# One exponential of 128x512 in place of four of 128x128, with the maxima subtracted on VectorE, in the first batch of an attention and expert-layer kernel

## Chip, core and metric

The kernel runs on one core of a Trainium2 chip. The metric is the device time of one execution in microseconds. TensorE (PE), VectorE (DVE), ScalarE (ACT), GpSimd (POOL) and SyncE (SP) run their own instruction queues in order and wait for one another by semaphores. Tiles lie in SBUF, results of TensorE in PSUM, in eight banks of 128 x 512 floats.

## The reference

```
x       = q, k times 64 ** -0.25                    # (4 batches, 8 heads, 576 rows, 64)
phi(x)  = exp(h - max(h)),  h = x @ omega.T - |x|^2/2    # 128 features, max over the features
kv, z   = sum over rows of phi(k) * v,  of phi(k)
attn    = phi(q) @ kv / (phi(q) @ z + 1e-6)
x       = attn as 2304 x 512
h = x @ w_in;  x = (h * clip(h + 3, 0, 6) / 6) @ w_out       # 512 -> 2048 -> 512
h = x @ w2_in; y = (h * sigmoid(1.702 h)) @ w2_out
```

The term |x|^2/2 is the same for all features of a row, so it falls out of h - max(h). The kernel therefore takes only the projection, its maximum over 128 features, and the exponential of the difference.

## The kernel before

The attention of one batch is a list of steps (`att_steps`, from L450). For each of eight heads: PJ (L330) projects 512 rows of k and q onto the features, PL (L313) does the same once per batch for the 64 leftover rows of all heads, QT (L366) transposes the query features on TensorE and copies them out (in batch 0 on VectorE, L372; later on ScalarE), KV (L341) sums phi(k) v into a bank that ScalarE copies to the tile `kv` (L363), NU (L377) multiplies the query features with kv (L386, L395) and normalizes on VectorE (`den`, `rden`, `xt`, L413 to L421), and XT (L429) transposes the result (L433) and splits it into a rounded high part on ScalarE (L279) and the rest on VectorE (L280).

A projection writes two banks, one for each half, each of 128 rows x 4 groups x 128 features (`project`, L282). `features` (L293) then takes the maximum over the features of each group, negated, on VectorE (L295), and makes four exponentials on ScalarE, one per group with its maximum as the bias (L297), from PSUM into the SBUF tile `e` (or `el` for the leftover rows). Both PJ and PL call it once per half. It gives back the last exponential and the reduction; the first weight conversion of the run is issued behind those of heads 4 and 5 (`att.feat`, L745), later ones behind `gate` or behind those of head 7.

Batch 0 runs alone at the start (L742). Its last twelve steps share the time with the first weight conversions: `convert_1` (L200) unpacks 64-bit weights by two ScalarE activations (L213, L215), three VectorE operations (`wmag`, `wtop`, `wpow`, L217 to L225) and one GpSimd product (L228); `convert_2` (L231) adds the parts on VectorE (L236) and splits them (L239, L240). Then the loop over chunks of the first expert layer begins (L807): `emit_h` (L513) and `emit_o` (L555) are TensorE's main work, the steps of batches 1 to 3 are put between them by `side`, and the second layer follows (`h_pair`, L856; `o_pair`, L1008).

The instructions of each engine are ordered by a planner that lists them by a timeline of its own costs, in order of emission where several are ready; only `behind` fixes an order by hand. An instruction at the head of an engine's queue that waits holds up all behind it.

Of the kernel before, what the change touches and what calls it, by code (L numbers as in the profile page):

```python
# [14 lines left out]
AF = mybir.ActivationFunctionType  # L15
ALU = mybir.AluOpType
AX = mybir.AxisListType
# [5 lines left out]
def performer_moe_kernel(  # L23
# [13 lines left out]
    nc = tc.nc  # L37
# [4 lines left out]
    B, NPAIR, P = qk.shape[:3]  # L42
# [3 lines left out]
    M = omega.shape[1]  # L46
# [62 lines left out]
    def bank(shape, name):  # L109
        n_ps[0] += 1  # L110
        if banks[0] == "acc" or banks[0] == "both" and n_ps[0] % 2:
            return acc.tile(shape, F32, tag="acc", name="acc")
        return psp.tile(shape, F32, tag="ps", name="ps")
# [84 lines left out]
    half = {}  # L198
# [47 lines left out]
    whole = {}  # L246
# [35 lines left out]
    def project(a, ps):  # L282

        last = None
        for n in range(4):
            for half in (1, 0):
                rows = HALVES[half]
                with behind(last):
                    last = nc.tensor.matmul(  # L289
                        out=ps[half][:, n, :], lhsT=a(rows, n), rhs=omt[rows, :], start=True, stop=True  # L290
                    )

    def features(ps, e):  # L293
        mx = at.tile([P, 4], F32, tag="mx", bufs=4, name="mx")
        dve = nc.vector.reduce_max(mx, ps, axis=AX.X, negate=True)  # L295
        for r in range(4):
            act = nc.scalar.activation(  # L297
                out=e[:, r, :], in_=ps[:, r, :], func=AF.Exp, bias=mx[:, r:r + 1]
            )
        return act, dve  # L300

    class Att:
# [10 lines left out]
        def PL(self):  # L313
            a, self.vl = lqkv.pop(self.b)
            self.el = at.tile([P, 2 * NPAIR, M], F32, tag="el", name="el")
            ps = [bank([P, NPAIR, M], "ps") for _ in HALVES]
            project(lambda rows, i: a[rows, i, :], ps)
            for j, p in enumerate(ps):
                features(p, self.el[:, j * NPAIR:(j + 1) * NPAIR])

        def QTL(self):
            ps = bank([P, NPAIR, P], "ps")
# [7 lines left out]
        def PJ(self, h):  # L330
            a = qkv[self.b, h // 2][0][:, h % 2]
            ps = [bank([P, R, M], "ps") for _ in HALVES]
            project(lambda rows, n: a[rows, n // 2, n % 2, :], ps)
            self.e[h] = at.tile([P, 2, R, M], F32, tag="e", bufs=2, name="e")
            for half, p in enumerate(ps):
                self.feat[h] = features(p, self.e[h][:, half])

        def feature(self, h, j, r):
            return self.e[h][:, r % 2, 2 * j + r // 2]
# [344 lines left out]
    ps = bank([P, 4, P], "ps")  # L684
    for n in range(WARM):
        nc.tensor.matmul(
            out=ps.rearrange("p a m -> p (a m)"),
# [557 lines left out]
```

## Time and profile before

| what | us |
|---|---|
| median of 3 runs (lowest, highest) | 902.18 (901.68, 904.79) |
| profiled execution | 906.58 |
| its span, first to last instruction | 904.8 |
| PE, DVE, ACT, POOL busy in the span | 886.0, 554.3, 478.0, 322.6 |

Times in views count from the span's first instruction. In a timeline a row gives start, duration, engine, line, operation, tiles, shape and count; in brackets stands how long the engine had been idle and what released it. A duration runs to the last write, and the next instruction of an engine can start a little before it ends, so the difference of two starts is what an instruction takes of its queue. Rows with a count are several merged. The busy time of PE is modelled. The granted clock of TensorE was 0.998 over the span.

### The profile page before, as it was taken

Reading aid. Unit: us, or ns where it says so; the run is one execution under the profiler, and the core shown is the slowest. Engines: PE = TensorE matmul, PEld = TensorE weight load, DVE = VectorE, ACT = ScalarE, POOL = GpSimd, SP = SyncE. Lnnn points to the kernel's source line nnn. Section 1 sums busy time; section 2 is a strip of 40 time slices with the busy share of each in tenths; the row PEclk is TensorE's granted clock in tenths of the full one; section 3 lists DMA queues with packets and bytes.
Section 4 is the critical chain, followed back from the end, with each engine's and each line's share of the span. In section 5 each row is a group of like instructions: output and inputs, shape, how many; then the busy total and the mean of one; then the engine's idle time right before and its main releaser. Section 6 shows DMA issues by size and latency. Waiting matters only on the chain.

```text
span 904.8 us, 16525 instructions
## 1 busy us (share of the span) xinstructions
PE 886.0 (98%) x6344; PEld 757.1 (84%) x6344; DVE 554.3 (61%) x952; ACT 478.0 (53%) x973; POOL 322.6 (36%) x257
## 2 busy tenths in 40 slices
PE   8899999999999999999999999999999999999998
PEld 6667777788788778878888888878999888899998
DVE  5887688473754736475573343666887343368785
ACT  5887677376664666656553343444545232245452
POOL 0122222044636565475673121877000243440000
PEclk9999999999999999999999999999999999999999
DMA  6677669698888987778857325999889644565562
GB/s 209 226 248 270 234 239 316 245 329 282 286 275 288 342 304 290 233 276 288 314 204 256 128 98 206 349 400 356 277 288 354 233 170 162 180 174 153 158 204 82
DMA packets 74416, 224.57 MB, mean 248 GB/s; under 512 B 7521, under 2 KB 13793, under 8 KB 74337
## 3 DMA queue, kind: packets, MB, share of 16 engines
q1 hardware_dynamic: 73872, 223.12, 71.1%
q8 instruction: 50, 0.82, 0.4%
q10 hardware_dynamic: 464, 0.39, 0.2%
q14 instruction: 30, 0.24, 0.1%
HBM read 160.57 MB, written 62.91 MB: 247 GB/s over the span
## 4 chain that ended last, share of the span: by engine, by line
PE 82%; DVE 8%; ACT 6%; issue 1%; POOL 1%; DMA 1%; DVEq 0%; SPq 0%; ACTq 0%; POOLq 0%
PE o L1008 19%; PE o L555 18%; PE ps L513 18%; PE h L856 16%; PE hl L873 3%; PE ps L289 2%; ACT e L297 2%; DVE w L236 2%; PE ps L386 1%; PE ps L347 1%; ACT wtop L213 1%; DVE mx L295 1%; DVE wtop L221 1%; PE ps L369 1%; DVE gs L530 1%
## 5 line engine op out<-in xcount | busy, mean ns | idle before, releaser
L513 PE MATMUL ps<-x,wss 128*128 128x512 f32 x768 | 195.5, 399 | 2.5 <-ACT el L297 1.1
L1008 PE MATMUL o<-wss,gs 128*128 128x256 f32 x1512 | 173.9, 277 | 0.2 <-DVE gs L977 0.2
L1008 PEld LDWEIGHTS o<-wss,gs 128*128 128x128 f32 x1512 | 173.4, 188 | 0.9 <-DVE gs L977 0.6
L513 PEld LDWEIGHTS ps<-x,wss 128*128 128x128 f32 x768 | 140.9, 189 | 35.0 <-ACT wss L239 3.1
L856 PE MATMUL h<-xo,wss 128*128 128x512 f32 x672 | 158.5, 391 | 0.9 <-DVE t L889 0.9
L856 PEld LDWEIGHTS h<-xo,wss 128*128 128x128 f32 x672 | 123.9, 188 | 27.5 <-DVE t L889 1.8
L228 POOL TENSOR_TENSOR w<-w,wpow 128x1024 f32<-128x1024 f32 x32 | 69.2, 2162 | 204.6 <-DVE wpow L225 166.7
L525 DVE SCALAR_TENSOR_TENSOR ga<-ga,ps 128x512 f32<-128x512 f32 x80 | 50.1, 632 | 121.1 <-ACT ga L524 121.1
L899 POOL TENSOR_TENSOR g<-g,c 128x512 f32<-128x512 f32 x48 | 64.7, 1349 | 164.0 <-ACT g L898 163.8
L976 ACT CAST gs<-g 128x512 fp32r<-128x512 f32 x112 | 69.6, 622 | 80.3 <-PE o L1008 49.3
L555 PE MATMUL o<-gs,wsh 128*128 128x512 f32 (+1 forms) x480 | 110.4, 374 | 1.2 <-ACT gs L529 1.0
L555 PE MATMUL o<-gs,wss 128*128 128x512 f32 (+1 forms) x480 | 109.5, 374 | 0.2 <-ACT gs L529 0.2
L253 POOL TENSOR_TENSOR wsn<-w,wsn 128x512 fp32r<-128x512 f32 x64 | 86.6, 1367 | 63.5 <-ACT wsn L252 63.5
L977 DVE TENSOR_TENSOR gs<-g,gs 128x512 fp32r<-128x512 f32 x112 | 79.9, 716 | 33.6 <-ACT gs L976 32.3
L524 ACT ACTIVATE ga<-ps,three 128x512 f32<-128x512 f32 x80 | 51.4, 650 | 86.5 <-PE ps L513 86.0
L555 PEld LDWEIGHTS o<-gs,wsh 128*128 128x128 f32 x480 | 82.2, 188 | 17.6 <-ACT gs L529 1.4
L555 PEld LDWEIGHTS o<-gs,wss 128*128 128x128 f32 x480 | 82.4, 188 | 15.8 <-ACT gs L529 0.4
L297 ACT ACTIVATE e<-ps,mx 128x128 f32<-128x128 f32 x220 | 61.1, 396 | 23.5 <-DVE mx L295 23.3
L530 DVE TENSOR_TENSOR gs<-ga,gs 128x512 fp32r<-128x512 f32 x80 | 62.5, 791 | 16.5 <-ACT gs L529 14.7
L898 ACT ACTIVATE g<-c 128x512 f32<-128x512 f32 x48 | 30.3, 632 | 60.2 <-DVE c L889 60.2
L529 ACT CAST gs<-ga 128x512 fp32r<-128x512 f32 x80 | 46.0, 580 | 27.8 <-DVE ga L525 27.4
L252 ACT CAST wsn<-w 128x512 fp32r<-128x512 f32 x64 | 38.3, 620 | 39.5 <-DVE w L236 13.2
(132 smaller groups left out, 1102.7 us busy)
## 6 DMA issues: line engine op xcount, KB each, us to landing
wss<-left SPq DMA_DIRECT2D x56, 512.0 KB, 3.9
wss<-ws0i SPq DMA_DIRECT2D x48, 512.0 KB, 4.9
wraw<-in_w_in_dram SPq DMA_DIRECT2D x32, 512.0 KB, 5.4
wraw<-in_w_out_dram SPq DMA_DIRECT2D x32, 512.0 KB, 6.3
left<-wsn SPq DMA_DIRECT2D x32, 512.0 KB, 3.7
wss<-ws0o SPq DMA_DIRECT2D x24, 512.0 KB, 4.6
ws0i<-wss SPq DMA_DIRECT2D x16, 512.0 KB, 3.3
wss<-sumsa SPq DMA_DIRECT2D x16, 512.0 KB, 3.5
```

The costliest lines, as they stand in the source:

```text
L228: nc.gpsimd.tensor_tensor(out=w, in0=w, in1=q, op=ALU.mult)
L253: nc.gpsimd.tensor_tensor(out=s[:, :, 1], in0=t, in1=s[:, :, 0].bitcast(F32), op=ALU.subtract)
L297: act = nc.scalar.activation(out=e[:, r, :], in_=ps[:, r, :], func=AF.Exp, bias=mx[:, r:r + 1])
L513: nc.tensor.matmul(out=ps, lhsT=w[:, wi, kk, :], rhs=x[:, xi, kk, :], start=(m == 0), stop=(m == 3 * NK - 1),)
L524: nc.scalar.activation(out=g, in_=ps, func=AF.Relu, bias=three)
L530: gate[1] = nc.vector.tensor_tensor(out=s[:, 1, :], in0=g, in1=s[:, 0, :].bitcast(F32), op=ALU.subtract)
L555: nc.tensor.matmul(out=ps[:, e, :], lhsT=w[:, wi, cols], rhs=s[:, gi, :], start=(c == 0 and m == 0 and e == 0), stop=(c == NC - 1 and m == ...
L856: nc.tensor.matmul(out=ps, lhsT=s[:, wi, q, :], rhs=xop[q, op][:, xi], start=(first and m == 0), stop=(m == 5), skip_group_check=not first,)
L899: mul = eng.tensor_tensor(out=g, in0=g, in1=src, op=ALU.mult)
L976: split_ins[0] = nc.scalar.copy(hi, g)
L977: split_ins[1] = nc.vector.tensor_tensor(out=lo, in0=g, in1=hi.bitcast(F32), op=ALU.subtract)
L1008: last_row[0] = nc.tensor.matmul(out=out, lhsT=s[:, gi, d * P:(d + 1) * P], rhs=w[:, wi, :], start=(start and m == 0), stop=(stop and m == 2),
```

## The change

In batch 0, for the second half of every projection (eight heads and the leftover rows), the reduction no longer negates, VectorE subtracts the broadcast maxima from the whole bank into the SBUF tile, and ScalarE makes one exponential of 128x512 there, in place. The first halves, and all of batches 1 to 3, stay as they are. What `features` gives back is then that exponential and the subtraction.

```diff
-    def features(ps, e):
+    def features(ps, e, whole=False):
         mx = at.tile([P, 4], F32, tag="mx", bufs=4, name="mx")
+        if whole:
+            nc.vector.reduce_max(mx, ps, axis=AX.X)
+            dve = nc.vector.tensor_tensor(
+                out=e, in0=ps, in1=mx.unsqueeze(2).to_broadcast([P, 4, M]), op=ALU.subtract
+            )
+            return nc.scalar.activation(out=e, in_=e, func=AF.Exp), dve
         dve = nc.vector.reduce_max(mx, ps, axis=AX.X, negate=True)
         for r in range(4):
...
             for j, p in enumerate(ps):
-                features(p, self.el[:, j * NPAIR:(j + 1) * NPAIR])
+                features(p, self.el[:, j * NPAIR:(j + 1) * NPAIR], self.b == 0 and j == 1)
...
             for half, p in enumerate(ps):
-                self.feat[h] = features(p, self.e[h][:, half])
+                self.feat[h] = features(p, self.e[h][:, half], self.b == 0 and half == 1)
```

## Rows read from the trace of the kernel before

**Rows 1.** Page, part 1: engine, busy us, share of the span, instructions.
```profile
PE 886.0 (98%) x6344; PEld 757.1 (84%) x6344; DVE 554.3 (61%) x952; ACT 478.0 (53%) x973; POOL 322.6 (36%) x257
```

**Rows 2.** Busy time by stretch: stretch, its length, busy us of each engine, clock, DMA.
```profile
5.28:42.00 36.72, 30.84 (x459) 25.39 (x458) 27.06 (x64) 27.21 (x88) 2.14 (x1) 1.00 0.67 226
42.00:60.00 18.00, 15.95 (x125) 11.21 (x126) 16.29 (x36) 14.24 (x30) 5.43 (x3) 1.00 0.83 279
60.00:80.00 20.00, 20.00 (x144) 16.18 (x143) 14.93 (x27) 17.31 (x40) 5.27 (x3) 1.00 0.66 229
```

**Rows 3.** The chain of waits in order of time: start us, us, what.
```profile
29.55 2.15 POOL w L228
...
53.28 0.73 PE ps L513 x2
```

**Rows 4.** Waits of PE from 0 to 60 us: us in total, times, longest.
```profile
PE acc L386 <- ACT kv L363: 3.0, 3, 1.5
...
PE acc L433 <- DVE den L413: 1.5, 2, 0.8
...
PE acc L289 <- ACT e L297: 0.6, 1, 0.6
```

**Rows 5.** Timeline of ScalarE, 0 to 60 us.
```profile
8.14 1.14 ACT L297 ACTIVATE e<-ps,mx 128x128 f32<-128x128 f32 x4 [6.13 <-DVE mx L295]
9.15 1.16 ACT L297 ACTIVATE e<-acc,mx 128x128 f32<-128x128 f32 x4
...
14.16 0.40 ACT L363 COPY kv<-acc 128x65 f32<-128x65 f32 x1
...
28.23 1.24 ACT L215 ACTIVATE w<-wraw 128x1024 f32<-128x1024 uint32 x1
...
39.33 1.21 ACT L213 ACTIVATE wtop<-wraw 128x1024 bf16<-128x1024 bf16 x1
40.38 2.21 ACT L215 ACTIVATE w<-wraw 128x1024 f32<-128x1024 uint32 x2
...
55.83 1.14 ACT L529 CAST gs<-ga 128x512 fp32r<-128x512 f32 x2
56.86 1.18 ACT L215 ACTIVATE w<-wraw 128x1024 f32<-128x1024 uint32 x1
```

**Rows 6.** Timeline of VectorE, 0 to 60 us.
```profile
7.41 0.69 DVE L295 TENSOR_REDUCE mx<-ps 128x4 f32<-128x512 f32 x1 [3.35 <-PE ps L289]
8.02 0.68 DVE L295 TENSOR_REDUCE mx<-acc 128x4 f32<-128x512 f32 x1
...
15.35 0.16 DVE L413 TENSOR_SCALAR den<-acc 128x4 f32<-128x4 f32 x1 [0.86 <-PE acc L386]
15.54 0.18 DVE L417 RECIPROCAL rden<-den 128x4 f32<-128x4 f32 x1
...
17.71 0.69 DVE L295 TENSOR_REDUCE mx<-ps 128x4 f32<-128x512 f32 x1 [0.94 <-PE ps L289]
...
21.71 0.69 DVE L280 TENSOR_TENSOR x<-acc,x 128x512 fp32r<-128x512 f32 x1 [0.80 <-ACT x L279]
...
25.22 0.69 DVE L295 TENSOR_REDUCE mx<-acc 128x4 f32<-128x512 f32 x1 [0.41 <-PE acc L289]
...
28.18 0.43 DVE L225 TENSOR_SCALAR wpow<-wtop 128x512 int32<-128x512 int32 x1
...
31.72 1.29 DVE L236 TENSOR_TENSOR w<-w,wtop 128x512 f32<-128x512 f32 x2 [0.72 <-POOL w L228]
...
36.54 1.28 DVE L295 TENSOR_REDUCE mx<-acc 128x4 f32<-128x512 f32 x2
```

**Rows 7.** Timeline of PE, 14 to 43 us.
```profile
14.61 0.69 PE L386 MATMUL acc<-kv,qpt 128*64 128x65 f32 x16 [0.81 <-ACT kv L363]
...
20.40 0.66 PE L433 MATMUL acc<-ident,xt 128*128 128x128 f32 x4 [0.78 <-DVE den L413]
...
42.75 0.69 PE L386 MATMUL acc<-kv,qpt 128*64 128x65 f32 x16 [1.52 <-ACT kv L363]
```

## Prediction

> **What bounds the kernel now.** I read the busy shares first, then the stretches, the chain of waits, the waits of the matmul engine, and last the timelines of ScalarE and VectorE in the first 60 us. TensorE is busy 98% of the span [rows 1]. The table by stretch says where that is untrue: between 60 and 80 us PE is busy all 20.00 us, but from 5.28 to 42 us it is busy 30.84 of 36.72, and from 42 to 60 it is busy 15.95 of 18.00 [rows 2]. So PE stands idle 5.88 + 2.05 = 7.9 us in the only stages that the change touches; from 53.28 us on the chain of waits runs on PE [rows 3]. Whatever the edit does must show as a change of these 7.9 us, since PE's own work stays the same.
>
> Those idle microseconds are shared by two engines [rows 4]. ScalarE is named for the product of query features and kv (L386), which waits 3.0 us in three places for the small copy kv, and for the exponentials, 0.6 us at L289 (the row shown) and as much at L369: 4.2 us together. VectorE is named for the transposes of L433, in two rows, 1.5 us (shown) and 1.1 us: 2.6 us. Over 5.28 to 42 us the two are loaded alike, VectorE 27.06 us and ScalarE 27.21 us [rows 2]. Neither is "the" bound: the chain passes from one to the other.
>
> **The change, part by part.** In batch 0 the function runs for eight heads and once for the leftover rows; its second half is taken each time, so nine groups change.
>
> Removed from ScalarE: 9 groups of four exponentials of 128x128. A group starts at 8.14 us and the next at 9.15 [rows 5], so four take 1.01 us of the queue (a single one lasts longer, but they overlap). Added: 9 exponentials of 128x512 from SBUF to SBUF. The nearest row is the cast of 128x512 out of SBUF: two start at 55.83 us and the next instruction at 56.86 [rows 5], so one takes 1.03 / 2 = 0.52 us of the queue. I take 0.53; the upper end is 0.57, half of the 1.14 us that the pair lasts with nothing overlapped. ScalarE gets 1.01 - 0.53 = 0.48 us less per group (0.44 at the upper end), 9 x 0.48 = 4.3 us in all (4.0 at that end).
>
> The Trainium skill, "ScalarE: Activation LUTs", section "What ACT_TABLE_LOAD costs", puts an activation with a pointer bias at 280 ns + 0.833 ns per element and the overlap of neighbours at 93 ns. By that, as an estimate, four of 128 columns would take 4 x (387 - 93) = 1.18 us, and the saving would be 0.57 to 0.66 us per group. This trace shows 1.01 us for four [rows 5], so its smaller saving stands in the sum.
>
> Added to VectorE: 9 subtractions of 128x512 with one operand in PSUM and the maxima broadcast. The subtraction at L280 has the same shape, PSUM on one side and SBUF on the other, and lasts 0.69 us [rows 6]; the reduction of the same tile lasts 0.69 us, and the next one starts 0.61 us after it [rows 6]. So an added subtraction takes about 0.60 us of the queue when it need not wait. It does need the maxima of the instruction before it: the reciprocal that needs the sum just before it starts 0.19 us after that one's start, though that one lasts 0.16 us [rows 6]; a dependent pair stands 0.03 us beyond the end of the first, so 0.72 us instead of 0.60 if nothing is put between. VectorE thus gets 9 x 0.60 = 5.4 us, at most 9 x 0.72 = 6.5 us. I take 0.60, since other reductions are ready in most places. The negation in the reduction falls away at no price, the instruction is the same.
>
> The Trainium skill, "VectorE: DVE Perf Modes", section "The DRAIN you can't avoid", says that a semaphore between chained VectorE operations costs nothing extra. By that rule the sum would keep 5.4 us and lose its upper end; the pair of rows above, 0.19 us for a 0.16 us operation, speaks against it, so the end of 6.5 us stays.
>
> Busy time from 5.28 to 42 us becomes 27.06 + 5.4 = 32.5 us on VectorE and 27.21 - 4.3 = 22.9 us on ScalarE, of 36.72. VectorE's idle pieces there that have a row are 0.86, 0.94, 0.80, 0.41 and 0.72 us [rows 6], 3.7 us that could take the subtractions if they fell just there. They do not all. I follow the chain:
>
> First heads, 8.14 to 14.61 us: ScalarE runs six groups without a gap, and kv starts only at 14.16 us behind them; the product of L386 starts at 14.61 [rows 5, 7]. After: ScalarE needs 3 x 1.01 + 3 x 0.53 = 4.6 us, but VectorE must deliver six reductions and three subtractions, 7.41 + 9 x 0.60 = 12.8 us, and the copy of the transposed features behind them (0.68 us). The product starts at about 13.6: 1.0 us earlier.
>
> 17.71 to 20.40 us: VectorE runs two reductions, a copy, den, rden, xt, and the transposes of L433 wait for it [rows 6, 7]. One subtraction lies ahead of the copy: +0.6. Net now 0.4 earlier. The next two reductions, at 25.22 us, wait for PE [rows 6], which starts from these transposes; so that is kept.
>
> 25.22 to 29.55 us: VectorE is busy from two reductions to wpow (28.18 + 0.43 = 28.6) [rows 6], ScalarE to the end of the weight activation L215 at 28.23 + 1.24 = 29.47 [rows 5], and GpSimd's product starts at 29.55 [rows 3]. ScalarE's end moves by -0.4 - 2 x 0.48 to about 28.1, VectorE's by -0.4 + 0.6 to 28.8. GpSimd starts at about 28.85: 0.7 earlier, and VectorE is what ends the wait now.
>
> 31.72 to 37.8 us: VectorE is back to back and takes one more subtraction: 0.1 earlier. At the last head, the reductions stand at 36.54 [rows 6]; the subtraction ends near 38.3, the exponential near 38.95, and the weight activation L213 that started at 39.33 [rows 5] starts 0.4 us earlier. From there to 53.28 us nothing of the change runs. The next weights follow that activation, so 0.4 us is what PE gets.
>
> Sum: profiled execution 906.58 us (span 904.8 plus 1.8 around it) less 0.4 is 906.2 us. The median of the runs shown is 902.18, 4.4 below that execution; the same difference gives **901.8 us**. The bounds: every subtraction on the chain and none of ScalarE's saving there is +6.5; all waits on ScalarE gone and every subtraction hidden is -4.2.
>
> **Rivals.** (a) ScalarE's queue is the real bound. For it: kv and the exponentials hold PE 4.2 us [rows 4], and the copies stand behind groups that halve. Against it: one of the three kv waits, 1.52 us at 42.75 us [rows 7], comes behind one L213 and two L215 that remain [rows 5]. 4.2 - 1.5 = 2.7 us would go: 899.5 us.
>
> (b) VectorE becomes the bound and the kernel is slower. Place: 25.2 to 37.8 us, where its idle is only 0.41 and 0.72 us [rows 6] and reductions, copies, weight conversions and normalization share it. Price: three subtractions for the heads 5 to 7 at 0.72, two more around 17.7 and 22.3 us that push the L433 transposes, so 5 x 0.72 = 3.6 us, less the 1.0 gained at the first heads: +2.6, 904.8 us. It decides when a subtraction is queued ahead of a copy or den that PE already waits for.
>
> (c) The edit does what it says but the planned order of the engines shifts elsewhere too, as the planner orders by its own times. The forecast keeps the order. A weight conversion ahead of a reduction costs as the 0.72 us before 31.72 [rows 6] does; four or five such places either way are +-3 us, 899 or 905.
>
> (d) ScalarE's exponential is no cheaper than four: then 9 x 0.48 returns to its queue, and only the subtractions count: nothing is gained at the first heads, and four of them stand on the chain, at 17.7, 25.2, 32.9 and 36.5 us: 4 x 0.6 = +2.4, 904.6 us. The casts of the same shape [rows 5] make this unlikely.
>
> **How the numbers follow.** Forecast, within some 1.3 us of no change: 0.50. (a) 0.17, (b) 0.17, (c) 0.12 shared evenly by both signs, (d) 0.04. Half a per cent, 4.5 us, is about what a measurement of this kernel can tell from no change; below 897.7 is faster, above 906.7 slower. Only the far ends of (a), (b) and (c) lie there. I give faster 0.12, same 0.75, slower 0.13. The likeliest case alone is 900.5 to 903.1. The range that holds the cases to 8 in 10 goes from 898.2 to 906.0.
>
> **What would show it.** Right: nine second-half exponentials of about 0.6 us in the first 40 us and nine subtractions of 0.69 us; ScalarE about 4.3 us less busy and VectorE 5.4 us more; the first product of L386 about 1 us earlier; GpSimd's first weight product released by VectorE; PE's idle in 5.28 to 60 us within 1.5 us of 7.9. Wrong: if kv no longer stops PE and the idle falls below 6 us (a), if L433 or L386 wait for VectorE by over 5 us (b), or if the difference arises behind 60 us (c).

## Result and profile after

| | before | changed |
|---|---|---|
| median of the runs, us | 902.74 (5 runs) | 908.56 (5 runs) |
| ratio, 95% interval | | 1.0054 (1.0041 to 1.0067) |
| profiled execution and its span, us | 906.58, 904.8 | 909.03, 907.2 |
| VectorE, ScalarE busy, us | 554.3, 478.0 | 563.5, 473.9 |

The change makes the kernel slower by half a per cent. The forecast was 901.8 us, 898.2 to 906.0. The two profiled executions lie only 2.4 us apart, the medians 5.8: the first profile of before holds a loss of 2.0 us near 320 us that a second profile of it does not have (the last section). So the experiments compare ratios, and profiles with one another up to 230 us.

The stretches of the changed kernel [rows 2 holds those of before]: stretch, length, busy time of PE, weight loads, VectorE, ScalarE, GpSimd, clock, DMA share, GB/s.

```profile
5.28:42.00 36.72, 31.81 (x458) 26.13 (x458) 31.75 (x71) 23.50 (x61) 2.13 (x1) 0.95 0.68 227
42.00:60.00 18.00, 13.71 (x122) 9.83 (x119) 15.42 (x35) 13.31 (x27) 4.27 (x2) 1.00 0.70 238
60.00:80.00 20.00, 20.00 (x144) 16.16 (x143) 13.64 (x25) 16.88 (x40) 6.20 (x3) 1.00 0.76 266
```

Up to 42 us, where all nine groups lie, VectorE has 4.7 us more and ScalarE 3.7 us less; 5.4 and 4.3 were forecast. But PE idles 18.00 - 13.71 = 4.3 us between 42 and 60 us, where it idled 2.05 before, and where only batch 0's last heads remain.

VectorE and ScalarE of the changed kernel at the first head [rows 5, 6], and PE's places [rows 7]; timelines, with the idle time before a row in brackets:

```profile
7.63 0.68 DVE L296 TENSOR_REDUCE mx<-acc 128x4 f32<-128x512 f32 x1
8.35 0.69 DVE L297 TENSOR_TENSOR e<-acc,mx 128x512 f32<-128x512 f32 x1
```

```profile
9.07 0.63 ACT L300 ACTIVATE e<-e 128x512 f32<-128x512 f32 x1 [0.18 <-DVE e L297]
9.67 1.14 ACT L303 ACTIVATE el<-ps,mx 128x128 f32<-128x128 f32 x4
...
39.30 0.63 ACT L300 ACTIVATE e<-e 128x512 f32<-128x512 f32 x1
39.84 1.13 ACT L213 ACTIVATE wtop<-wraw 128x1024 bf16<-128x1024 bf16 x1
```

```profile
13.62 0.69 PE L392 MATMUL acc<-kv,qpt 128*64 128x65 f32 x16
...
29.46 0.63 PE L439 MATMUL ps<-ident,xt 128*128 128x128 f32 x4 [2.33 <-DVE den L419]
...
55.70 0.73 PE L519 MATMUL ps<-x,wss 128*128 128x512 f32 x2 [1.40 <-ACT wss L239]
```

The subtraction lasts 0.69 us, and directly behind its reduction it starts 0.72 us after it; this exponential takes 0.60 us of the queue (9.07 to 9.67), the one ahead of the last row 0.54. The first product with kv (L392, formerly L386) starts at 13.62, where the prediction had 13.6. The last row is the new thing: the second chunk's matmuls (L519, formerly L513) wait 1.40 us for the cast of their weights. Two rows of ScalarE's timeline of the changed kernel show why:

```profile
53.87 1.26 ACT L530 ACTIVATE ga<-ps,three 128x512 f32<-128x512 f32 x2 [1.27 <-PE ps L519]
55.03 0.62 ACT L239 CAST wss<-w 128x512 fp32r<-128x512 f32 x1
```

The cast stands in the queue behind two activations of the first chunk. In the kernel before, the cast came first and the activations second:

```profile
52.60 0.62 ACT L239 CAST wss<-w 128x512 fp32r<-128x512 f32 x1 [1.08 <-DVE w L236]
53.13 1.26 ACT L524 ACTIVATE ga<-ps,three 128x512 f32<-128x512 f32 x2
```

Nothing in the edit touches either. The planner has placed them anew.

The order of the two kernels can be laid side by side. Told apart by operation, tile and shape, as the traces name them, the last 871 instructions of ScalarE (in the kernel before, those from the first `ga` on) differ at 58 places, the last 856 of VectorE (from the first store of `gs` on) at 106, and SyncE's 465 DMA issues at 24. It is the same work, permuted.

### The profile page after: what moved, and what is told of

Read it like the earlier page. It is cut to its first block, busy times and chain, and to the rows that moved or that the text cites. A ratio compares the mean times of both kernels' runs of the same rounds, so it can differ in the third digit from the quotient of the medians.

```text
span 907.2 us, 16508 instructions
## 1 busy us (share of the span) xinstructions
PE 884.7 (98%) x6344; PEld 756.8 (83%) x6344; DVE 563.5 (62%) x961; ACT 473.9 (52%) x946; POOL 322.5 (36%) x257
## 4 chain that ended last, share of the span: by engine, by line
PE 81%; DVE 9%; ACT 6%; issue 2%; POOL 1%; DMA 1%; DVEq 0%; ACTq 0%; POOLq 0%
PE o L1014 19%; PE ps L519 19%; PE o L561 18%; PE h L862 14%; PE ps L289 3%; PE hl L879 2%; DVE w L236 2%; ACT wtop L213 1%; PE ps L392 1%; PE ps L353 1%; DVE mx L301 1%; DVE gs L536 1%; PE ps L375 1%; ACT e L303 1%; DVE wtop L221 1%
## 5 line engine op out<-in xcount | busy, mean ns | idle before, releaser
L519 PE MATMUL ps<-x,wss 128*128 128x512 f32 x768 | 194.2, 397 | 4.4 <-ACT wss L239 2.5
L519 PEld LDWEIGHTS ps<-x,wss 128*128 128x128 f32 x768 | 139.7, 188 | 36.0 <-ACT wss L239 3.5
L303 ACT ACTIVATE e<-ps,mx 128x128 f32<-128x128 f32 x212 | 58.0, 385 | 23.8 <-DVE mx L301 23.8
```

What stands on the lines that cost most here:

```text
L303: act = nc.scalar.activation(out=e[:, r, :], in_=ps[:, r, :], func=AF.Exp, bias=mx[:, r:r + 1])
L519: nc.tensor.matmul(out=ps, lhsT=w[:, wi, kk, :], rhs=x[:, xi, kk, :], start=(m == 0), stop=(m == 3 * NK - 1),)
```

## Experiments

Theory 1: the subtractions in VectorE's queue delay PE (rival b). Theory 2: the planner's new order behind the first chunk costs (rival c, with one sign). Theory 3, asked of `no_sub`, `early` and `late`: the fall of TensorE's clock to half behind the 2.33 us wait (shown in the last section). Each kernel was timed beside the kernel before on the same chip; the table at the end has all ratios.

**Taking the change apart.** `no_sub` leaves out the subtraction, so the exponentials are of h itself:

```diff
-            dve = nc.vector.tensor_tensor(...)
-            return nc.scalar.activation(out=e, in_=e, func=AF.Exp), dve
+            return nc.scalar.activation(out=e, in_=ps, func=AF.Exp), dve   # dve: the reduction
```

> In batch 0 the second halves get one exponential of 128x512 straight from PSUM and no subtraction: the maxima are taken but not subtracted, so the output is another. ScalarE keeps its saving of 9 x 0.4 us, VectorE gets nothing more. Theory 1 (the nine subtractions in VectorE's queue cause the loss): faster than before, by 1 to 3 us, 900 to 902 us; PE does not wait 2.3 us for den before the transposes of L439. Theory 2 (any change of the first batch makes the planner lay out the chunks behind 60 us anew, and that costs): 905 to 909 us like the changed kernel. Theory 3 (the fall of TensorE's clock after the 2.33 us wait at 27 us): no wait, no fall, about 903.

Measured: 1.0028 (1.0017 to 1.0039). Slower than before, with no work added anywhere. Theory 1 alone cannot give this. PE still waited for den before the second transposes:

```profile
PE ps L436 <- DVE den L416: 2.2, 1, 2.2
```

(waits of PE in `no_sub`, 0 to 50 us: total, times, longest.) So that wait does not need the subtractions. Theory 3 stays open here: the granted clock fell in this kernel too, to 0.50 from 28 to 34 us.

`sub_four` keeps the subtraction and makes four exponentials:

```diff
-            return nc.scalar.activation(out=e, in_=e, func=AF.Exp), dve
+            for r in range(4):
+                act = nc.scalar.activation(out=e[:, r, :], in_=e[:, r, :], func=AF.Exp)
+            return act, dve
```

> The subtraction stays on VectorE, but ScalarE makes four exponentials of 128x128 from the difference as before: VectorE's 5.4 us are added and ScalarE saves nothing. Theory 1: at least as slow as the changed kernel, 909 to 912 us, since the loss is VectorE's. If ScalarE's saving was hiding part of the loss, 911 to 913. Theory 2: no relation to the changed kernel's time, anything from 903 to 911.

Measured: 1.0046 (1.0031 to 1.0061), not slower than the changed kernel; its 908.13 us lies under theory 1's range.

`early` and `late` make the change in a part of the groups:

```diff
-  self.b == 0 and half == 1)
+  self.b == 0 and half == 1 and h < 4)      # early; late: h >= 4, and not for the leftover rows
```

> The change for the leftover rows and heads 0 to 3 only; heads 4 to 7 as before. Theory 1 with its place at 25 to 40 us, where VectorE runs without a gap: the loss goes, 901.5 to 904 us, the first product of L392 about 1 us earlier, and PE waits about 1 us, not 2.3, for the second transposes of L439. Theory 2: still 905 to 909 us. Theory 3: no clock below 1.0 at 30 us.

> The change for heads 4 to 7 only; the leftover rows and heads 0 to 3 as before. Theory 1: the whole loss and no gain at the first heads, 907 to 910 us, a wait of 2 us or more for den before the second transposes of L439. Theory 3: the clock falls at about 30 us again. Theory 2: anything from 903 to 910 us.

Measured: 1.0046 (1.0032 to 1.0061) and 1.0053 (1.0037 to 1.0069). Each half of the change costs as much as the whole, which theory 1 does not allow for `early`. The orders behind the first chunk turned out to be one and the same in these two, and other than in the changed kernel. This pointed to theory 2, and to a way to test it: the order is known before a kernel runs, so groups can be chosen by it.

`early` also bears on theory 3. In its profile PE waited 1.06 us before the second transposes, not 2.33, and the clock was 1.00 from 28 to 36 us (it fell later, at 43 us), yet the loss is there. `late` had the wait (2.35 us), the fall (0.57 from 30 to 34 us) and the loss, as theories 1 and 3 expected of it and theory 2 allowed.

**Work and order apart.** With the change in heads 0, 1, 2, 4, 7 and the leftover rows, alone or together, the order behind the first chunk stays that of before, place by place. Head 3, 5 or 6 alone turns it over.

```diff
-  self.b == 0 and half == 1)
+  self.b == 0 and half == 1 and h in (0, 1, 2, 4, 7))    # six_groups, with the leftover rows
+  self.b == 0 and half == 1 and h in (3,))               # head3; head6 likewise
```

> The change for the leftover rows and heads 0, 1, 2, 4 and 7: six of the nine groups. With these six the planner leaves the order of all engines from the first chunk of the expert layer on as in the kernel before. Theory 1 (the subtractions in VectorE's queue cost): two thirds of the changed kernel's +5 us, 906 to 908 us against 903.6 of before. Theory 2 (the loss is the new order behind 50 us, which the kernels run so far all have in one form or another): as before within 1.5 us, 902 to 905 us, and PE does not wait 1.4 us for wss at 53 us.

> The change for head 3 alone: one group of nine, 0.6 us more on VectorE, 0.5 us less on ScalarE. With it the planner lays out the engines' order behind the first chunk anew, the same layout as in the kernels with the change in heads 0 to 3 or in heads 4 to 7. Theory 1: a ninth of the loss, within 1 us of before. Theory 2: nearly the whole loss, 906.5 to 909 us, with the 1.4 us wait for wss at 53 us and waits of about 0.9 us near 97, 107, 124 and 140 us.

> The change for head 6 alone. The planner makes a third layout behind the first chunk, unlike that of before and that of head 3. Theory 1: within 1 us of before. Theory 2: another draw; if the order of before was a good one among many, 904.5 to 909 us.

Measured: six_groups 1.0000 (0.9992 to 1.0009); head3 1.0056 (1.0041 to 1.0072); head6 1.0040 (1.0026 to 1.0054). Two thirds of the work in the old order cost nothing; a ninth of it in a new order costs most or all of the loss. ScalarE of `six_groups` has the cast first again:

```profile
52.40 0.62 ACT L239 CAST wss<-w 128x512 fp32r<-128x512 f32 x1 [1.08 <-DVE w L236]
52.93 1.26 ACT L530 ACTIVATE ga<-ps,three 128x512 f32<-128x512 f32 x2
```

and `head3` has its wait of PE like the changed kernel:

```profile
56.55 0.73 PE L519 MATMUL ps<-x,wss 128*128 128x512 f32 x2 [1.42 <-ACT wss L239]
```

To leave no room for the number of groups, `nine_kept` adds first halves of heads 0, 1 and 2 to the six (nine groups, old order), and `head5_first` makes the change on the first half of head 5 alone (one group, the changed kernel's order but for a few matmul places and two of VectorE).

```diff
-  self.b == 0 and half == 1)
+  self.b == 0 and h in ((0, 1, 2), (0, 1, 2, 4, 7))[half])    # nine_kept, with the leftover rows
+  self.b == 0 and h in ((5,), ())[half])                      # head5_first
```

> Nine groups as in the change, but others: second halves of the leftover rows and of heads 0, 1, 2, 4 and 7, first halves of heads 0, 1 and 2. As many subtractions and exponentials of 128x512 as the change makes, in a choice with which the planner keeps the order of before from the first chunk on. Theory 1 (the subtractions cost): +4 to +5 us, 907 to 908.5 us. Theory 2 (the new order costs): as before within 1.5 us, 902 to 905 us.

> The change on the first half of head 5 alone: one group. The planner then lays out everything behind the first chunk as in the changed kernel (six of 5434 matmul places differ). Theory 1: within 1 us of before, 902.5 to 904 us. Theory 2: most of the changed kernel's loss, 906 to 908.5 us.

Measured: nine_kept 1.0008 (0.9999 to 1.0018), head5_first 1.0035 (1.0024 to 1.0046).

The kernels that keep the order leave out heads 3, 5 and 6, and heads 5 and 6 are where rival (b) had its place. For those the kernels with one and the same new order speak: `late`, with heads 4 to 7, lost no more (1.0053) than head 3 alone (1.0056).

`copies_35` is the changed kernel with two copies on ScalarE, its order otherwise untouched; `before_ga` has none of the change, only one edge:

```diff
-            if self.b == 0:
+            if self.b == 0 and h not in (3, 5):          # copies_35: heads 3 and 5 copy on ScalarE
...
-                nc.scalar.copy(s[:, 0], wj)
+                with behind(ga_act[0] if (kind, c) == ("i", 1) else None):    # before_ga
+                    nc.scalar.copy(s[:, 0], wj)
```

> The changed kernel, with the copies of the transposed features of heads 3 and 5 (0.6 us each) moved from VectorE to ScalarE, so that VectorE is relieved between 18 and 28 us; the order behind the first chunk is that of the changed kernel, place by place. Theory 1: 1 to 2 us faster than the changed kernel, 906.5 to 907.5 us, and the wait of 2.33 us at 27 us shrinks. Theory 2: within 1 us of it, 907.5 to 909 us.

> The kernel before with none of the change, but with ScalarE's cast of the second chunk's weights ordered by hand behind the first chunk's ga, as the planner puts it in all kernels with a new order. The planner then makes another layout still. Theory 1: only the wait for wss at 53 us is new, 1.4 us: 904 to 905 us. Theory 2: 905 to 909 us, with waits of 0.6 to 2 us between 95 and 175 us that before has not.

Measured: copies_35 1.0032 (1.0019 to 1.0045), before_ga 1.0033 (1.0021 to 1.0045).

`copies_35` came out at 907.18 us, in theory 1's range and just under theory 2's, so theory 2 missed here. But the wait that was to shrink went only from 2.33 to 2.15 us. The run leaves room for a price of the groups beside that of the order ("The remainder" below).

`before_ga`, an untouched first batch with one edge, is as slow as a new layout. It was no clean test of the order: the edge moved much else, PE's wait for the cast became 1.8 us, and the clock fell just there (granted clock 0.57 from 50 to 58 us). All six executions have a mean clock of 0.994 to 0.996, where the 76 of the kernel before have 0.997 to 1.000. How much of its loss is the clock's was not separated. Its other expected waits, 0.6 to 2 us behind 95 us, are there twice, 0.7 and 0.9 us.

**The clock apart.** Each execution has its mean granted clock on record, so the fall of the clock can be taken out. At a clock of 1.000, so with next to no fall, the one-group kernel (`head5_first` above, and `one_group` below, which is the same) took 906.24 us in the mean of 11 executions, and the kernel before, on the same two chips, 903.69 in 14: 2.55 us, 0.0028 of it. For `early` the difference at 1.000 is 3.6 us (2 executions against 5), for `no_sub` 1.7 (5 against 5), for `six_groups` -0.3 (5 against 4). So the loss of orders A, B and D (the letters of the table below) does not come from the clock. `sub_four`, `head3`, `head6`, `late` and `before_ga` have no execution at 1.000.

**Where the new order loses.** Busy time of PE from 95 to 175 us, the columns as above, in the kernel before (its second profile), `six_groups`, `head5_first`, the changed kernel and `head3`:

```profile
95.00:175.00 80.00, 78.17 (x566) 60.20 (x561) 57.64 (x122) 52.18 (x100) 17.18 (x8) 1.00 0.76 262
```

```profile
95.00:175.00 80.00, 78.16 (x569) 60.26 (x566) 57.76 (x122) 52.25 (x101) 17.19 (x8) 1.00 0.75 262
```

```profile
95.00:175.00 80.00, 76.60 (x565) 58.91 (x565) 60.49 (x125) 52.45 (x101) 17.74 (x9) 1.00 0.77 270
```

```profile
95.00:175.00 80.00, 76.49 (x565) 58.59 (x564) 59.86 (x125) 52.31 (x100) 18.70 (x9) 1.00 0.77 267
```

```profile
95.00:175.00 80.00, 75.41 (x559) 58.03 (x558) 58.23 (x123) 53.86 (x104) 20.28 (x9) 1.00 0.81 270
```

The first two agree to 0.01 us, the next two to 0.11; between the pairs lie 1.6 us, though `head5_first` has one group of the change and `six_groups` six. Who makes PE wait, 50 to 200 us, in `six_groups` and in the changed kernel:

```profile
PE o L561 <- ACT gs L535: 1.1, 2, 1.0
PE ps L519 <- ACT wss L239: 0.7, 2, 0.4
PE acc L439 <- DVE den L419: 0.7, 1, 0.7
PE ps L519 <- ACT x L279: 0.3, 1, 0.3
```

```profile
PE ps L519 <- ACT wss L239: 2.5, 3, 1.4
PE o L561 <- ACT gs L535: 1.2, 2, 0.9
PE ps L392 <- ACT kv L369: 0.6, 1, 0.6
PE ps L519 <- DVE wss L240: 0.5, 1, 0.5
PE acc L439 <- DVE den L419: 0.5, 1, 0.5
PE ps L519 <- ACT x L279: 0.3, 1, 0.3
```

The sums are 2.8 and 5.6 us: the casts of weights and a copy of kv come later relative to the matmuls that need them.

**The remainder.** The changed kernel's 1.0054 stood above head5_first's 1.0035 of nearly the same order. Both were run once more on one chip, as `all_nine` and `one_group`:

> The changed kernel itself, beside the one-group kernel of the same order. If the nine groups cost something of their own before the first chunk: 1 to 2 us slower than the one-group kernel, ratio to before 1.005. If only the order costs: within 0.5 us of the one-group kernel, 1.0035.

> The change on the first half of head 5 alone, with the changed kernel's order behind the first chunk. Ratio to before 1.0035 again, whichever holds for the nine groups; if it comes out at 1.005, the difference seen was the chip's.

Measured: 1.0048 (1.0030 to 1.0066) and 1.0037 (1.0023 to 1.0051): 0.0011 apart, about 1 us, with overlapping intervals. It points to a price of the nine groups of their own, but does not settle it. The clock is a rival here: none of the 12 executions of the changed kernel was at 1.000, 11 of the 23 of the one-group kernel were; at 0.998 the changed kernel took 908.2 us (10 executions) and the one-group kernel 909.2 (6).

All kernels, with the time at which the first matmul of the second product starts (`o`, L555 before), and from there to the 231st of the 768 matmuls of the first product (`ps<-x,wss`), from the PE timelines of single profiles. At that matmul the changed kernel is 4.1 us behind the second profile of before, and at the last of the 768 it is 4.5 us behind. The letters A to F name the new orders; F was made by hand.

| kernel | groups | order behind the first chunk | first o, us | from there, us | ratio |
|---|---|---|---|---|---|
| before, second profile | 0 | old | 57.60 | 127.8 | 1 |
| six_groups | 6 | old | 57.75 | 127.7 | 1.0000 |
| nine_kept | 9 | old | 59.05 | 127.8 | 1.0008 |
| head5_first / one_group | 1 | A | 59.27 / 58.74 | 129.2 / 129.4 | 1.0035 / 1.0037 |
| changed / all_nine | 9 | A | 60.07 / 60.53 | 129.4 / 129.4 | 1.0054 / 1.0048 |
| copies_35 | 9 | A | 59.15 | 129.3 | 1.0032 |
| head3 | 1 | B | 60.92 | 130.8 | 1.0056 |
| early / late | 5 / 4 | B | 59.29 / 59.03 | 130.6 / 130.5 | 1.0046 / 1.0053 |
| head6 | 1 | C | 59.62 | 129.5 | 1.0040 |
| no_sub / sub_four | 9 | D / E | 59.09 / 61.00 | 129.6 / 129.5 | 1.0028 / 1.0046 |
| before_ga | 0 | F | 63.00 | 125.8 | 1.0033 |

The stretch behind the first o depends on the order alone: 127.7 to 127.8 us in the old one, 129.2 to 129.4 in A, 130.5 to 130.8 in B. (In F the first o stands two places earlier among the matmuls, and starts 5.4 us later, behind the wait and the slow clock above.) Order A thus costs 1.6 us there and the 1.4 us for the cast before it, 3.0 us, which is 0.0033 of 904 us, close to the ratios of the one-group kernel, 1.0035 and 1.0037.

## Why the prediction was wrong

The step that failed is the one put as "The forecast keeps the order", behind rival (c). (c) was given 0.12 and both signs, with a price of 3 us either way. It was the main cause, worth about 3 us (2.55 at full clock) of the 4.3 to 4.9 that the ratios 1.0048 and 1.0054 give, and in all six new orders that ran the sign was the same. About 1 to 2 us stay open: the nine groups themselves, or the clock.

With it fell the premise "Whatever the edit does must show as a change of these 7.9 us". It rests on the reading that the chain of waits runs on PE from 53.28 us on, and that reading was wrong. From 133.00 to 145.14 us the chain of the kernel before runs on ScalarE and VectorE; three of its rows there:

```profile
133.73 2.18 ACT e L297 x8
...
138.00 1.08 ACT wtop L213
...
144.41 0.69 ACT wss L239
```

ScalarE's and VectorE's places count there too, and from 95 to 175 us order A cost PE 1.6 us.

- *Price per instruction, and both engines' sums.* Right, if a little high in the sums: 0.69 us, 0.72 us when dependent, 0.54 to 0.60 for the exponential (0.53 was taken), +4.7 and -3.7 us up to 42 us where 5.4 and 4.3 were forecast.
- *First heads.* Right: 13.62 against 13.6.
- *25 to 29.5 us.* Wrong: GpSimd started at 29.68 us, not 28.85. VectorE did not end that wait, ScalarE still did, as three rows of the changed kernel's chain of waits show (start, us, what):

```profile
27.95 0.63 ACT e L300
28.58 1.03 ACT w L215
...
29.68 2.14 POOL w L228
```

  The weight activation L215 stands behind the exponential, which had to wait for its subtraction (27.24 to 27.92): what ScalarE saved, it spent waiting. PE came earlier and waited 2.33 us where it had waited 1.06, and its clock fell (below). L213 started at 39.84, not 38.95. So PE's idle time from 5.28 to 60 us came to 4.9 + 4.3 = 9.2 us; that this lies within 1.5 us of 7.9, as a sign of being right asked, is no support, since 1.4 us of it is the cast's.
- *"From there to 53.28 us nothing of the change runs ... so 0.4 us is what PE gets".* Wrong for this kernel: the first o is 2.1 us later than in the first profile of before (57.94 to 60.07), of which 1.4 us is the wait for the reordered cast.
- *The chain's net of about zero.* Borne out by the kernels that keep the order, 1.0000 and 1.0008, for groups other than heads 3, 5 and 6. The steps that the chain counts for those were not tested in the old order, and one of them, 25 to 29.5 us, failed.
- *Rival (b),* VectorE as the bound, +2.6 us. Not the main cause: nine groups in the old order cost 0.7 us, at most 1.6 (0.9999 to 1.0018), and heads 4 to 7 in order B no more than head 3. In order A the nine may cost 1 to 1.7 us (1.0048 less 1.0037, 1.0054 less 1.0035), and taking 1.2 us off VectorE there (copies_35) came out at 1.0032; these intervals overlap.

Why the planner turns the order over for heads 3, 5 and 6 and not for the others was not tried.

## What to carry over

Where a planner orders the queues by its own timeline, an edit of half a microsecond is two edits: its own work, and a new order of everything behind it. Compare the built order first, and judge the edit in a variant that keeps it: here the edit was worth nothing that could be told from zero in the variants that kept the order, and a new order cost some 3 us. A fresh order deserves a chance of its own in a forecast, and where little idle time is left to lose, one on the slow side; here all six that ran lost 0.28 to 0.56%. They are not six independent draws: all six have the cast behind `ga`, with a wait of 1.4 us or more for it, and the sixth was made by hand.

## What was not expected of the hardware

TensorE's granted clock came down to half (1.2 of 2.4 GHz) for a few microseconds at a time, mostly behind a wait, and not in every execution. In the changed kernel it fell after the 2.33 us wait; two rows of PE's timeline and one of the table by stretch:

```profile
31.82 1.13 PE L392 MATMUL acc<-kv,qpt 128*64 128x65 f32 x16
32.89 1.03 PE L375 MATMUL ps<-ident,e 128*128 128x128 f32 x4
```

```profile
30.00:35.00 5.00, 5.00 (x60) 4.21 (x59) 3.85 (x7) 2.95 (x7) 1.81 (x1) 0.66 0.58 211
```

The same sixteen matmuls took 0.69 us elsewhere. The Trainium skill, "TensorE: Matmul & The Clock Gate", "Part 1: The HAM clock gate (the "warmup" mystery)", says that the point at which the clock rises behind the first matmuls varies between runs of one kernel. The profiles show the like of a fall, which comes in one execution and stays away in another. The one-group kernel has a fall from 321 to 325 us in one profile and none in the other, and the kernel before fell near 318 us in its first profile alone. With a wait of 1.7 us at the place above, the clock fell in nine_kept and not in six_groups, and behind a wait of 1.11 us near 318 us it fell in the first profile of before and not in the changed kernel's. Their rows for that stretch, before and changed:

```profile
300.00:345.00 45.00, 43.15 (x285) 33.98 (x284) 26.54 (x38) 29.99 (x65) 25.11 (x20) 0.96 0.87 316
```

```profile
300.00:345.00 45.00, 43.05 (x290) 34.03 (x289) 26.39 (x40) 32.46 (x71) 25.06 (x21) 1.00 0.90 321
```

The changed kernel's lag behind before shrinks from 3.75 to 2.26 us across this stretch (the matmuls of the first product that start at 304.51 and 308.26 us, and at 335.03 and 337.29). A second profile of before was taken to see whether its fall stays:

> The kernel before once more, for a second profile of it. If the stretch at half clock that its first profile shows at 318 us comes and goes between executions, this one has it elsewhere or not at all, and its span is 1 to 2 us shorter, 902 to 903 us.

Measured: 904.16 us, span 902.4, with no fall there, but one between 43 and 48 us (0.66). Its matmuls of the two places above start at 304.34 and 332.83 us, so the first profile lost 2.0 us between them, with the fall. The fall between 43 and 48 us left no such mark: the first o stands at 57.60 us there and at 57.94 in the first profile, which had none. And over the 76 executions of before, the 23 at a clock of 1.000 took 903.6 us and the 47 at 0.998 or less 903.7. So what a fall costs hangs on its place, a single profile of this kernel is uncertain by some 2 us, and a forecast worked from one profile's path carries that too.
